# A fused linear-attention and gated-MLP layer on one core: state products in runs of four token tiles, and SBUF buffers cut into other sizes

## The chip, the core and the metric

The kernel runs on one core of one Trainium2 chip. The metric is the device time of one execution in microseconds (us). The core has five engines that run at the same time, each through its own instructions in order: TensorE (PE in the profile, its weight loads PEld), VectorE (DVE), ScalarE (ACT), GpSimd (POOL) and SyncE (SP, which here only issues DMA transfers). They wait for one another through semaphores.

## The reference, cut to what matters

One layer over x of 2048 tokens x 512 features (float32). A layer norm feeds two branches, whose product is added to x:

```
xn = layernorm(x)
q, k, v = xn @ wqkv                        # 32 heads of 16
phi(t) = [softmax(t @ w_phi), softmax(-t @ w_phi)]      # 32 features a head
kv = sum over tokens of phi(k)^T v;  z = sum over tokens of phi(k)
o  = phi(q) kv / (phi(q) z + 1e-6)
s  = o @ wo
gate, up = xn @ W_gate, xn @ W_up          # 1376 hidden features
h  = relu(gate) * up
out = x + s * silu(h @ W_down)
```

So no token's attention can be finished before the sums kv and z ("the state") over all 2048 tokens are complete.

## The kernel before, in words

**Tiles.** There are N = 16 token tiles of 128 tokens, numbered n in the order in which they are worked on (line 225: blocks 2 and 3 by turns, then 0 and 1). The kernel normalizes a tile (norm_*), turns it with TensorE (turn, transpose_x) and keeps it as two numbers of reduced precision, a high and a low part, in XT. Every large product is made of three: low x high, high x low, high x high (mm3, line 204). Products of two blocks are combined from sums of blocks (A11 to A22 and S1 to S4, line 48), so seven products do the work of eight.

**First part: keys, values, state.** Tiles 0 and 1 have code of their own (lines 1253 to 1293). Then pair(m) for m = 1 to 7 (line 1295) works on n = 2m and 2m + 1: key products (PSUM banks py and px, called pk in the profile; from pair 3 on `px` first takes a copy of `py`, the ACT instruction pk<-pk of line 1310, and TensorE writes on after it), value products (pv), the features of the keys (exponents, exp_all, features_k: subtract maxima, exp, sum, reciprocal, multiply; tile ek), the query products of a tile (query, line 421, bank pq; stored to DRAM as pq<-pqs), and in each pair the *state products* of the two tiles before, n - 2 and n - 1 (kv_products, lines 1376 to 1378 and 512). kv_products takes 16 small products for one tile, each on a quarter of the array (tile_position, 32 columns), all into one PSUM bank, PKV (pkv). Its operands ek and v can be written over only after it. features_split also adds ek to a sum in DRAM with a POOL DMA (zacc<-ek). After pair 7, state() (line 1426) takes the products of the last two tiles, copies the bank (kvacc, ACT), turns it (DVE) and spreads it into kvt.

**Second part: the hidden features.** The hidden size is cut into 11 feature tiles f. f_prep(f) (line 557) takes the raw weights of one tile (rawg, rawd, loaded by f_load, line 535: three DMAs on SP), forms their sums on POOL (tab), rounds high parts on ACT (wa, wb, wc, wd, fdh) and takes low parts on POOL, and stores all nine tiles to DRAM (put, ws<-...) for the second half of the tokens. At its end it loads the next tile's raw weights (line 611). gate_up_apart and gate_up (lines 757 and 708) make the seven block products of one feature tile; down makes the products with W_down. Two halves of 1024 tokens run one after the other. Between these products, q_pair and q_back work through the queries: stored queries are loaded from DRAM (q_load, line 851, tiles pql), turned, exponentiated and multiplied with the state (bank pnum). One column of query products (q_tile, line 640) uses weight sums that POOL and ACT make in q_sums (line 616) during pair 3 and 4. Last come the products with wo (out_tile).

**What sets the order.** Each engine's instructions keep the order in which the program issues them. The order of side work (f_prep, q_sums, all_queries, stores through pace.when) comes from Clock (line 68): it estimates when TensorE and the other engines are free, and pump() issues the next step of a generator when its operands should be there. f_prep(0) starts at pair 7, f_prep(1) after it (START, line 40); all_queries, which begins with state(), starts 30 blocks after the pairs (line 1502). PLAN (line 39) sets by hand where weight sums are made. SP issues DMAs in order: one that waits holds all behind it.

**Buffers.** SBUF tiles come from three sets that the whole kernel shares: u8 (8 KB a partition, B8 = 3), u4 (4 KB, B4 = 8) and u2 (2 KB, B2 = 40; line 31). A tile gets a buffer that is free, or its first writer waits until one is. In u8: the raw weights wkT, wvr, wqT, then th, rq, tq, the results y of two blocks, of2. In u4: zacc, ek, two weight sums, eq and ez of the queries, o and of. In u2: the attention weights, xt, v, and the feature tiles.

Of the kernel before, what the change touches and what calls it, by code (L numbers as in the profile page):

```python
# [13 lines left out]
P = 128  # L14
S = 2048
D = 512
# [3 lines left out]
KD = D // P  # L20
NF = -(-F // P)
# [4 lines left out]
NP = 8  # L26
CHUNKS = [(0, 1), (2, 3), (4, 5), (6, 7), (8, 9, 10)]
PAIRS = [(2, 3), (0, 1)]
B8, B4, B2 = 3, 8, 40
LEAD = 3  # L30
QUERIES = [(0, 1, 2), (6, 7, 4, 5, 3)]

# [7 lines left out]

START = (14, 15)
TURN = 9
KV_END = ()
SUMS = 5
WO_WITH = (4, 5, 6, 7)
DOWNS = {2: 1, 4: 1, 6: 1, 7: 1}
# [118 lines left out]
def layer_kernel(ctx: ExitStack, tc: tile.TileContext, x, wkT, wqT, wv, wo, wf, cst, out):  # L165
    pace = Clock()
    nc = InOrder(tc, pace)
# [81 lines left out]
    def fold_queries(*ks):  # L249

        ps_ = [ps((P, 2, KD, 64), name="pfold") for _ in range(2)]
        for i, k in enumerate(ks):
            for j in range(KD):
                for r in range(2):
                    rr = slice(64 * r, 64 * r + 64)
                    nc.tensor.matmul(ps_[r][:, i, j, :], wq_raw[rr, k, j * P:(j + 1) * P], bd_sb[rr, j, rr],
                                     start=i == 0 and j == 0, stop=True, skip_group_check=True, tile_position=(64 * r, 0))

        def parts(k):
            for r in range(2):  # L260
                split(*(t.rearrange("p (j r x) -> p r j x", r=2, x=64)[:, r] for t in WQ[k]), ps_[r][:, ks.index(k)])
        return [lambda k=k: parts(k) for k in ks]
# [246 lines left out]
            nc.sync.dma_start(to, flat(phi))  # L509
        PHI[n] = phi  # L510

    def kv_products(n):

        phi, v = PHI.pop(n).rearrange("p (j a c) s f -> p c j a (s f)", a=2, c=4), VH.pop(n)
        v = v.rearrange("p (c j x) -> p c j x", c=4, j=4)
        if n == 0:
            PKV.append(ps((P, 8, 64), name="pkv"))
        for j in range(4):
            for c in range(4):
                r = slice(32 * c, 32 * c + 32)  # L520
                nc.tensor.matmul(PKV[0][r, j], v[:, c, j], phi[:, c, j], start=n == 0 and j == 0,
                                 stop=n == N - 1, skip_group_check=True, tile_position=(0, 32 * c))
# [31 lines left out]
    def put(f, i, t):  # L554
        pace.when(t, lambda: nc.sync.dma_start(wspill[f][i], f32(flat3(t))))

    def f_prep(f, keep=True):


        rg, rd, tab = RAW.pop(f)  # L560
        b11, b12, b21, b22 = (rg[c][:, :, s, :] for c in range(2) for s in range(2))
        ta, tb = tab or two("tab", True)
        yield "gpsimd", b22
        add(nc.gpsimd, tb[:, 0], b12, b11, ALU.subtract)
        add(nc.gpsimd, ta[:, 1], b22, b12, ALU.subtract)
        if keep:
            wa, wb = w_pair("wa"), None
        else:
            t = u8((P, 4, 2, 2, P), "wab", F32R)
            wa, wb = (t[:, 0], t[:, 1]), (t[:, 2], t[:, 3])  # L570
        yield "scalar", b11
        for c in range(2):
            nc.scalar.activation(wa[0][:, c], rg[c][:, :, 0, :], AF.Copy)
        put(f, 0, wa[0])
        yield "gpsimd", ta
        add(nc.gpsimd, ta[:, 0], b22, tb[:, 0], ALU.subtract)
        add(nc.gpsimd, tb[:, 1], b21, ta[:, 0], ALU.subtract)
        wb = wb or w_pair("wb")
        yield "scalar", ta
        nc.scalar.activation(wb[0], ta, AF.Copy)  # L580
        put(f, 2, wb[0])
        for c in range(2):
            yield from sums_of(wa[1][:, c], rg[c][:, :, 0, :], f32(wa[0][:, c]), ALU.subtract, wa[0])
        put(f, 1, wa[1])
        wc = w_pair("wc")
        yield "scalar", tb
        nc.scalar.activation(wc[0], tb, AF.Copy)
        put(f, 4, wc[0])
        yield from sums_of(wb[1], ta, f32(wb[0]), ALU.subtract, wb[0])
        put(f, 3, wb[1])  # L590
        wd = u2((P, 2, 2, P), "wd", F32R)
        yield "scalar", b22
        nc.scalar.activation(wd[:, 0], b22, AF.Copy)
        yield from sums_of(wc[1], tb, f32(wc[0]), ALU.subtract, wc[0])
        put(f, 5, wc[1])
        fd = u2((P, D), "fdh", F32R), u2((P, D), "fdl", F32R)
        yield "scalar", rd
        nc.scalar.activation(fd[0], rd, AF.Copy)
        put(f, 7, fd[0])
        yield "gpsimd", wd  # L600
        add(nc.gpsimd, wd[:, 1], b22, f32(wd[:, 0]), ALU.subtract)
        put(f, 6, wd)
        yield from sums_of(fd[1], rd, f32(fd[0]), ALU.subtract, fd[0])
        put(f, 8, fd[1])
        if keep:
            FT[f], WD[f] = [wa, wb, wc, wd], fd
            nxt = f + 1
            while nxt in AHEAD:
                nxt += 1
            del rg, rd, ta, tb, tab  # L610
            if nxt < NF:
                f_load(nxt)
        DONE.add(f)
        yield None,

    def q_sums(q):

        t = u8((P, 4, 2, 2, P), "rq")
        r, ta, tb = [t[:, k] for k in range(2)], t[:, 2], t[:, 3]
        for k in range(KD):  # L620
            h, l = (f32(x[:, 256 * q:256 * q + 256].rearrange("p (d x) -> p d x", d=2)) for x in WQ[k])
            yield "gpsimd", WQ[k][1]
            add(nc.gpsimd, r[k // 2][:, k % 2], h, l)
        b11, b12, b21, b22 = (t[:, :, d, :] for t in r for d in range(2))
        o = u8((P, 2, 2, 2, 2, P), "tq", F32R)
        yield "gpsimd", r[1]
        add(nc.gpsimd, tb[:, 0], b12, b11, ALU.subtract)
        add(nc.gpsimd, ta[:, 1], b22, b12, ALU.subtract)
        yield "gpsimd", ta
        add(nc.gpsimd, ta[:, 0], b22, tb[:, 0], ALU.subtract)  # L630
        add(nc.gpsimd, tb[:, 1], b21, ta[:, 0], ALU.subtract)
        for i, x in enumerate((ta, tb)):
            yield "scalar", x
            nc.scalar.activation(o[:, i, 0], x, AF.Copy)
            yield from sums_of(o[:, i, 1], x, f32(o[:, i, 0]), ALU.subtract, o)
        TQ[q] = o
# [366 lines left out]
    def o_load(q):  # L1003
        LOADED.add(q)
        for u, parts in enumerate(UNITS):
            if q in [part[0] for part in parts]:
                pace.finish(BACK[u])
                for g in STORES.pop(u, []):
                    pace.finish(g)
        qs = QUERIES[q > QUERIES[0][-1]]  # L1010
        if q == qs[0]:

            t = u8((P, 2, 4, 256), "of2")
            OF[q], OF[qs[1]] = t[:, 0], t[:, 1]
            del t
        if q not in OF:
            OF[q] = u4((P, 4, 256), "of")
        nc.sync.dma_start(OF[q], OD[q])
        for t in (2 * q, 2 * q + 1):
            if t in yspill:  # L1020
                YK[t] = u2((P, D), "yk")
                nc.sync.dma_start(YK[t], yspill[t])
# [65 lines left out]
        return t  # L1088


    wk_raw, wv_raw, wq_raw = u8((P, KD, D), "wkT"), u8((P, KD, D), "wvr"), u8((P, KD, D), "wqT")
    bd_sb = u2((P, KD, P), "cb")
    ident = sb.tile([P, P], F32, name="ident")
    load_x(0)
# [20 lines left out]
        add(nc.gpsimd, by_parity(WV[k][1]), even_first(wv_raw[:, k, :]), f32(by_parity(WV[k][0])), ALU.subtract)  # L1115
    norm_vector(0)

    nc.vector.memset(wq_raw[:, 0, 0:1], 0.0)
    nc.sync.dma_start(wq_raw[:, 0:2, :], wqT[:, 0:2, :])
    nc.sync.dma_start(wv_raw[:, 0:2, :], wv[:, 0:2, :])  # L1120
    nc.sync.dma_start(wq_raw[:, 2:4, :], wqT[:, 2:4, :])
    load_x(2)
    nc.sync.dma_start(wv_raw[:, 2:4, :], wv[:, 2:4, :])
    for n in range(3, 7):
# [170 lines left out]
    def pair(m):  # L1295
# [77 lines left out]
        pace.pump()  # L1373
        features_split(n)
        t_steps(m, "split a")
        if m not in KV_END:
            kv_products(n - 2)
            kv_products(n - 1)
        pace.pump()
        if seven:  # L1380
            block(px, A22, T[3], False)
# [17 lines left out]
        if not seven:  # L1399
            features_v(n, va)  # L1400
        EB.append((eb, px))
        if m in KV_END:
            kv_products(n - 2)
            kv_products(n - 1)
        query(n)
        t_steps(m, "end")
        pace.pump()

    EB, MULT = [], [(None, None), (nc.gpsimd, nc.gpsimd)]
    for m in range(1, NP):  # L1410
        pair(m)
# [7 lines left out]
    nc.vector.memset(ones, 1.0)  # L1419
    kvt = sb.tile([P, NG, 32], F32, tag="kvt", bufs=1, name="kvt")  # L1420
    nc.vector.memset(kvt, 0.0)
    q_load(0)
    query(N - 1)
    pace.pump()

    def state():
        nonlocal kvacc
        kv_products(N - 2)
        kv_products(N - 1)

        kvacc = u2((P, 256), "kvacc")
        nc.scalar.activation(kvacc, PKV[0][:, :4].rearrange("p j x -> p (j x)"), AF.Copy)
        yield "vector", kvacc
        kvT = ps((P, 256), name="kvT")
        nc.vector.transpose(kvT, kvacc)
        kvT = kvT.rearrange("p (j x f) -> p j x f", x=4, f=DH)
        kvacc = None
        for c in range(4):
            r, h = slice(32 * c, 32 * c + 32), c % 2
            nc.vector.tensor_copy(kvt[r, :, DH * h:DH * h + DH].rearrange("p (j a) f -> p j a f", a=2), kvT[r, :, 0:4:3, :])  # L1440
        yield None,
# [22 lines left out]
    def all_queries(half):  # L1464
        nonlocal zs
        if not half:
            yield from state()
            zs = pace.add(normalizers(), first=True)
            yield 24,
        for u, parts in enumerate(UNITS):  # L1470
            if parts[0][0] in QUERIES[half]:
# [161 lines left out]
```

## Time and profile before

| | |
|---|---|
| median of 3 runs | 546.84 us (546.66 to 548.46) |
| the profiled execution's own time | 546.74 us |
| its span, first to last instruction | 545.0 us |
| granted TensorE clock | 1.00 |
| PE busy | 539.6 us (99%) |
| DVE, POOL, ACT busy | 372.4, 366.9, 258.7 us |
| moved by DMA | 125.98 MB |

How to read the lines: a group's or a timeline's row names the engine, the operation, what it writes <- what it reads by the program's tile names, the shape, and xN for N instructions. Numbers in front of it in the timeline are the start and the length in us from the span's start; [0.56 <-ACT pk] is idle time of that engine before the row and what ended it, inferred from semaphores. L64 is the helper through which every instruction is issued, so tiles identify the work. Matmuls overlap in the pipeline: their length is more than the distance between two starts, and the starts tell the pace.

### The profile page before, as it was taken

Reading aid. Unit: us, or ns where it says so; the run is one execution under the profiler, and the core shown is the slowest. Engines: PE = TensorE matmul, PEld = TensorE weight load, DVE = VectorE, ACT = ScalarE, POOL = GpSimd, SP = SyncE. Lnnn points to the kernel's source line nnn. Section 1 sums busy time; section 2 is a strip of 40 time slices with the busy share of each in tenths; the row PEclk is TensorE's granted clock in tenths of the full one; section 3 lists DMA queues with packets and bytes.
Section 4 is the critical chain, followed back from the end, with each engine's and each line's share of the span. In section 5 each row is a group of like instructions: output and inputs, shape, how many; then the busy total and the mean of one; then the engine's idle time right before and its main releaser. Section 6 shows DMA issues by size and latency. Waiting matters only on the chain.

```text
span 545.0 us, 9140 instructions
## 1 busy us (share of the span) xinstructions
PE 539.6 (99%) x3186; PEld 440.5 (81%) x3186; DVE 372.4 (68%) x585; ACT 258.7 (47%) x462; POOL 366.9 (67%) x328
## 2 busy tenths in 40 slices
PE   9999999999999999999999999999999999999997
PEld 8898888877887888787887888887777887878886
DVE  5988778677768338789883442899999494924323
ACT  3788767654435564545434240334354545342510
POOL 1569999767787999899896235262365765842591
PEclk9999999999999999999999999999999999999999
DMA  8339789555899957887869998692664735657073
GB/s 283 147 129 326 177 215 237 133 131 107 197 284 391 334 179 275 301 298 272 289 242 337 412 414 313 240 366 73 223 200 135 275 112 166 221 186 277 0 233 115
DMA packets 76367, 125.98 MB, mean 231 GB/s; under 512 B 6689, under 2 KB 29089, under 8 KB 75425
## 3 DMA queue, kind: packets, MB, share of 16 engines
q1 hardware_dynamic: 74160, 117.99, 61.7%
q0 software_dynamic: 2016, 7.34, 7.7%
q8 instruction: 25, 0.41, 0.3%
q14 instruction: 22, 0.17, 0.1%
q10 hardware_dynamic: 144, 0.07, 0.0%
HBM read 68.49 MB, written 52.69 MB: 222 GB/s over the span
## 4 chain that ended last, share of the span: by engine, by line
PE 90%; DVE 6%; issue 1%; DMA 1%; POOL 1%; ACT 0%; DVEq 0%; POOLq 0%; ACTq 0%
PE py L64 20%; PE pd L64 10%; PE pa L64 10%; PE pk L64 9%; PE pb L64 9%; PE pso L64 8%; PE pc L64 6%; PE pq L64 6%; PE pv L64 5%; PE pkv L64 2%; PE pfold L64 1%; PE pnum L64 1%; PE pxT L64 1%; DVE qs L64 1%; DMA wb<-ws 1%
## 5 line engine op out<-in xcount | busy, mean ns | idle before, releaser
L64 PE MATMUL py<-fdh,hl 128*128 128x512 f32 x176 | 69.1, 392 | 0.0
L64 PE MATMUL py<-fdl,hh 128*128 128x512 f32 x176 | 68.5, 389 | 0.0
L64 PE MATMUL py<-fdh,hh 128*128 128x512 f32 x176 | 68.5, 389 | 0.0
L64 PE MATMUL pa<-XT,wa 128*128 128x512 f32 x264 | 67.3, 390 | 0.0
L64 PEld LDWEIGHTS pa<-XT,wa 128*128 128x128 f32 x264 | 49.4, 188 | 11.1 <-POOL tab L64 0.4
L64 DVE TENSOR_TENSOR y<-py,y 128x512 f32<-128x512 f32 x40 | 27.5, 689 | 31.4 <-PE py L64 31.3
L64 POOL TENSOR_TENSOR hl<-t,hh 128x512 fp32r<-128x512 f32 x16 | 20.7, 1295 | 39.5 <-ACT hh L64 39.5
L64 POOL TENSOR_TENSOR y<-y,ys 128x512 f32<-128x512 f32 x24 | 30.9, 1292 | 17.9 <-ACT ys L64 17.4
L64 PEld LDWEIGHTS py<-fdh,hl 128*128 128x128 f32 x176 | 33.0, 188 | 8.8 <-issue 1.2
L64 PEld LDWEIGHTS py<-fdh,hh 128*128 128x128 f32 x176 | 33.0, 188 | 6.9
L64 POOL TENSOR_TENSOR ez<-eq,zB 128x1024 f32<-128x1024 f32 x16 | 38.5, 2412 | 0.1
L64 PEld LDWEIGHTS py<-fdl,hh 128*128 128x128 f32 x176 | 33.0, 188 | 6.7
L64 PE MATMUL pd<-XT,wd 128*128 128x512 f32 x132 | 33.9, 392 | 0.2
L64 PE MATMUL pd<-XT,wc 128*128 128x512 f32 x132 | 33.9, 391 | 0.0
L64 PE MATMUL pb<-XT,wb 128*128 128x512 f32 x132 | 33.6, 390 | 0.0
L64 POOL TENSOR_TENSOR ol<-of,oh 128x512 fp32r<-128x512 f32 (+1 forms) x13 | 19.8, 1548 | 20.3 <-ACT oh L64 20.3
L64 ACT ACTIVATE hh<-t 128x512 fp32r<-128x512 f32 x16 | 10.1, 633 | 49.3 <-DVE t L64 48.1
L64 PE MATMUL pc<-XT,wb 128*128 128x512 f32 x132 | 33.5, 389 | 0.0
L64 DVE TENSOR_REDUCE mx<-pk 128x32 f32<-128x512 f32 x32 | 20.5, 683 | 16.6 <-PE pk L64 16.5
L64 PE MATMUL pq<-XT,wqh 128*128 128x512 f32 (+1 forms) x112 | 30.6, 360 | 0.0
L64 DVE TENSOR_TENSOR pb<-pb,t 128x512 f32<-128x512 f32 x16 | 11.1, 696 | 28.4 <-ACT pd L64 28.3
L64 PE MATMUL pk<-wkh,XT 128*128 128x512 f32 x88 | 30.3, 396 | 0.0
(203 smaller groups left out, 1456.6 us busy)
## 6 DMA issues: line engine op xcount, KB each, us to landing
xts<-XT SPq DMA_DIRECT2D x4, 1792.0 KB
zacc<-ek POOLq DMA_DIRECT2D x14, 512.0 KB, 5.5
XT<-xts SPq DMA_DIRECT2D x7, 1024.0 KB
rawg<-wf SPq DMA_DIRECT2D x22, 256.0 KB
ws<-wa SPq DMA_DIRECT2D x22, 256.0 KB
ws<-wb SPq DMA_DIRECT2D x22, 256.0 KB
ws<-wc SPq DMA_DIRECT2D x22, 256.0 KB
wa<-ws SPq DMA_DIRECT2D x22, 256.0 KB
```

The lines of the kernel that those rows point to most:

```text
L64: return self.tc.keep_in_program_order(op(*a, **k))
```

## The change

It has four parts.

1. KV_AT = (2, 4, 6) replaces KV_END = (). The state products are taken only in pairs 2, 4 and 6, there for all tiles since the last time (four), and in state() for the last four. KV_FROM holds the first tile not yet taken.
2. Buffers: u8 from 3 to 2, u4 from 8 to 10, u2 stays 40; 56 KB in both. The raw query weights wqT become two u4 tiles of half the size, rq with its sums (q_sums) becomes two u4 tiles, and the first two tiles of loaded attention output in each half (of2) become two u4 tiles.
3. f_load(1) is issued inside f_prep(0), behind the store of the first rounded weights, no longer at its end.
4. q_load(0), which stood ahead of query(N - 1) and so ahead of state(), stands behind state() and the start of normalizers().

```
-B8, B4, B2 = 3, 8, 40
+B8, B4, B2 = 2,10,40
-KV_END = ()
+KV_AT = (2,4,6)
...
-                    nc.tensor.matmul(ps_[r][:, i, j, :], wq_raw[rr, k, j * P:(j + 1) * P], bd_sb[rr, j, rr],
+                    nc.tensor.matmul(ps_[r][:, i, j, :], wq_raw[k // 2][rr, k % 2, j * P:(j + 1) * P], bd_sb[rr, j, rr],
...
-    def kv_products(n):
+    def kv_products(*ns):
+        for n in ns:
+            kv_product(n)
+
+    def kv_product(n):
...
         put(f, 0, wa[0])
+        if f == 0:
+            f_load(1)
...
-            if nxt < NF:
+            if nxt < NF and nxt not in RAW:
                 f_load(nxt)
...
-        t = u8((P, 4, 2, 2, P), "rq")
-        r, ta, tb = [t[:, k] for k in range(2)], t[:, 2], t[:, 3]
+        r, (ta, tb) = (two(x, False) for x in ("rq", "tab"))
...
-            t = u8((P, 2, 4, 256), "of2")
-            OF[q], OF[qs[1]] = t[:, 0], t[:, 1]
-            del t
+            for k in qs[:2]:
+                OF[k] = u4((P, 4, 256), "of")
...
-    wk_raw, wv_raw, wq_raw = u8((P, KD, D), "wkT"), u8((P, KD, D), "wvr"), u8((P, KD, D), "wqT")
+    wk_raw, wv_raw, wq_raw = u8((P, KD, D), "wkT"), u8((P, KD, D), "wvr"), [u4((P, 2, D), "wqT") for _ in range(2)]
...
-        if m not in KV_END:
-            kv_products(n - 2)
-            kv_products(n - 1)
+        if m in KV_AT:
+            kv_products(*range(KV_FROM.pop(), n))
+            KV_FROM.append(n)
...
-        if m in KV_END:
-            kv_products(n - 2)
-            kv_products(n - 1)
...
-    q_load(0)
     query(N - 1)
...
     def state():
         nonlocal kvacc
-        kv_products(N - 2)
-        kv_products(N - 1)
+        kv_products(*range(KV_FROM[0], N))
...
             yield from state()
             zs = pace.add(normalizers(), first=True)
+            q_load(0)
             yield 24,
```

More of the change, by code (lines that the diff above doesn't have):

```diff
@@ L1116, in layer_kernel @@
     norm_vector(0)
-    nc.vector.memset(wq_raw[:, 0, 0:1], 0.0)
-    nc.sync.dma_start(wq_raw[:, 0:2, :], wqT[:, 0:2, :])
+    nc.vector.memset(wq_raw[0][:, 0, 0:1], 0.0)
+    nc.sync.dma_start(wq_raw[0], wqT[:, 0:2, :])
     nc.sync.dma_start(wv_raw[:, 0:2, :], wv[:, 0:2, :])
-    nc.sync.dma_start(wq_raw[:, 2:4, :], wqT[:, 2:4, :])
+    nc.sync.dma_start(wq_raw[1], wqT[:, 2:4, :])
     load_x(2)
@@ L1407, in pair @@
         pace.pump()
+    KV_FROM = [0]
     EB, MULT = [], [(None, None), (nc.gpsimd, nc.gpsimd)]
```

## The prediction

> **What bounds the kernel now.** I read the page first, its span and the engines' totals.
>
> ```profile
> span 545.0 us, 9140 instructions
> PE 539.6 (99%) x3186; PEld 440.5 (81%) x3186; DVE 372.4 (68%) x585; ACT 258.7 (47%) x462; POOL 366.9 (67%) x328
> ```
>
> TensorE is the bound, nearly without a gap, and the change takes no matrix product away. So it can win only what TensorE loses between products: at a change of tile shape, or at a short wait for another engine. To find those I read the waits of the weight loads, then everything that touches the state's bank pkv.
>
> ```profile
> PEld pkv L64 <- issue: 2.6, 8, 0.4
> PEld pd L64 <- DVE t L64: 1.0, 2, 0.5
> PEld pk L64 <- ACT pk L64: 0.8, 2, 0.6
> ```
>
> The largest entry is the state product itself: eight times, once before each run of small products, the weight load sits idle with nothing to wait for. A run is 64 records (two for each of 32 products) for two token tiles. All other waits are under 0.6 us.
>
> **Part 1: eight runs become four.** KV_AT = (2, 4, 6) leaves out the runs of pairs 1, 3, 5 and 7; those of pairs 2, 4, 6 and of state() take four tiles. The number of products stays; four times less TensorE goes into and out of them. The price of one such passage is in the timeline of TensorE around the first run:
>
> ```profile
> 39.19 0.40 PE L64 MATMUL pq<-XT,wqh 128*128 128x256 f32 x2
> 39.52 1.10 PE L64 MATMUL pkv<-ek,v 128*32 128x64 f32 x64
> 40.55 0.50 PE L64 MATMUL pk<-wkh,XT 128*128 128x512 f32 x1
> 40.89 0.40 PE L64 MATMUL pk<-wkl,XT 128*128 128x512 f32 x1
> 41.13 0.63 PE L64 MATMUL pk<-wkh,XT 128*128 128x512 f32 x2
> ```
>
> The pq products before start every 0.12 us (the row of two lasts 0.40, one of them 0.28), the last at 39.31, so the next start was due at 39.43 and came at 39.52: 0.09 lost. From the first to the last start of the run are 1.10 - 0.22 = 0.88 us for 63 steps, 0.014 each; at that pace the next start was due at 40.42 and came at 40.55: 0.13 lost. The first pk product then holds its successor for 0.34 instead of 0.24: 0.10 lost. Sum 0.32. The chain, in order of time, gives the same with other numbers (pair 4's run):
>
> ```profile
> 95.28 1.03 PE pkv L64 x64
> 96.31 1.58 PE pk L64 x6
> 97.89 1.36 PE pv L64 x6
> ```
>
> 1.03 against 64 x 0.014 = 0.90 is 0.13, and six products in 1.58 instead of 1.36 are 0.22: 0.35. I take 0.34, four times: **-1.36 us**. Bounds: the least is that only the entry goes and the exit grows with the run, 4 x 0.09 = 0.4 us; the most is 4 x 0.35 = 1.4.
>
> The Trainium skill has a rule that speaks against part of this: "TensorE: Matmul & The Clock Gate", section "The cost: per-tile semaphore tail", says that the tail behind a pack of tiled products grows by some 26 ns with each one that signals a semaphore. Two more signalling products in each of the four longer runs would give back about 0.2 us by that estimate. All runs here have the same length, so no row shows it.
>
> **Part 2: where the moved products land.** The 0.90 us of products taken out of pairs 1, 3, 5, 7 are done one pair later. That is neutral where TensorE is the bound, but not at its two waits for ACT (pk<-pk copies a key block aside before TensorE may write on):
>
> ```profile
> 133.21 0.58 ACT L64 ACTIVATE pk<-pk 128x512 f32<-128x512 f32 x1
> 133.32 0.39 PE L64 MATMUL pv<-h,XT 128*128 128x512 f32 x1
> 133.84 0.19 PEld L64 LDWEIGHTS pk<-h,XT 128*128 128x128 f32 x1 [0.56 <-ACT pk L64]
> 133.84 0.50 PE L64 MATMUL pk<-h,XT 128*128 128x512 f32 x1
> 134.18 0.40 PE L64 MATMUL pk<-l,XT 128*128 128x512 f32 x1
> ```
>
> From 133.32 to 133.84 are 0.52 us instead of 0.227 (6 products in 1.36), and the next step is 0.34: 0.29 + 0.11 = 0.40 lost. ACT is late because the exponents before it on ACT come from DVE, and in this stretch DVE has little idle time:
>
> ```profile
> 122.00:134.00 12.00, 11.87 (x114) 9.48 (x113) 10.70 (x17) 6.06 (x10) 8.28 (x9) 1.00 0.43 78
> ```
>
> (PE 11.87, PEld 9.48, DVE 10.70 us busy of 12.) Pair 6's run lies in this stretch and gets two tiles more, 0.90 us of work for TensorE exactly where it waits 0.29 us later. The wait is filled: **-0.40**. The bounds are -0.40 and 0.
>
> The other side is pairs 3, 5 and 7, which get 1.24 us shorter (0.90 + 0.34): ACT and DVE must follow. At the start of pair 6 they just keep up now:
>
> ```profile
> 115.11 1.29 DVE L64 TENSOR_REDUCE mx<-pk 128x32 f32<-128x512 f32 x2 [0.82 <-PE pk L64]
> 118.83 0.60 ACT L64 ACTIVATE pk<-pk 128x512 f32<-128x512 f32 x1
> 119.25 0.39 PE L64 MATMUL pv<-h,XT 128*128 128x512 f32 x1
> 119.48 0.50 PE L64 MATMUL pk<-h,XT 128*128 128x512 f32 x1
> ```
>
> TensorE starts at 119.48, one regular step after 119.25, with the copy done at 119.43. With TensorE 1.24 us earlier, DVE can begin mx only 0.82 earlier (its idle time), so exponents and copy come 0.8 to 1.0 earlier: a new wait of 0.2 to 0.4, of which I take **+0.2**. At pair 4 the copy has more room:
>
> ```profile
> 86.68 0.58 ACT L64 ACTIVATE pk<-pk 128x512 f32<-128x512 f32 x1 [0.47 <-PE pk L64]
> ```
>
> ACT idles 0.47 there, and TensorE has a block of 1.36 us between what the copy reads and what waits for it: 0 to 0.2, I take **+0.1**. In pair 7 DVE idles longer before it and nothing is added.
>
> **Part 3: the second feature tile's raw weights.** f_load(1) moves from the end of f_prep(0) to behind its first store. Its three DMA issues leave SP here and go behind ws<-wa:
>
> ```profile
> 133.57 0.45 SPq L64 DMA_DIRECT2D ws<-wa  x1
> 141.01 0.32 SPq L64 DMA_DIRECT2D ws<-wb  x1
> ...
> 144.31 2.78 SPq L64 DMA_DIRECT2D pql<-pq  x2
> ...
> 149.11 1.64 SPq L64 DMA_DIRECT2D rawg<-wf  x2
> ```
>
> SP issues nothing from 134.0 to 141.0; two issues of 1.64 us together and a third of half of that fit there, so the new place costs nothing (without that cover: some 2.5 us later stores, which nobody reads before the second half). What it gains shows one stage on:
>
> ```profile
> 154.66 1.44 POOL L64 TENSOR_TENSOR tab<-rawg 128x256 f32<-128x256 f32 x2 [0.98 <-DMA rawg<-wf]
> 156.84 0.63 ACT L64 ACTIVATE wb<-tab 128x512 fp32r<-128x512 f32 x1 [0.88 <-POOL tab L64]
> 159.02 0.58 ACT L64 ACTIVATE t<-pa 128x512 f32<-128x512 f32 x1
> 161.09 0.72 DVE L64 STREAM_TRANSPOSE pq<-pql 128x512 f32<-128x512 f32 x1
> 162.32 1.52 PE L64 MATMUL pc<-XT,wc 128*128 128x512 f32 x6
> 163.05 0.68 DVE L64 TENSOR_TENSOR e<-pd,e 128x512 f32<-128x512 f32 x1
> 163.84 1.22 PEld L64 LDWEIGHTS pd<-XT,wd 128*128 128x128 f32 x6 [0.43 <-POOL fdl L64]
> 163.88 1.63 PE L64 MATMUL pd<-XT,wd 128*128 128x512 f32 x6
> ```
>
> POOL waits 0.98 for the transfer. Its sums feed ACT's roundings of that tile; wb waits 0.88 for them and stands with others in front of t<-pa. That copy comes at 159.02, DVE follows, and its e<-pd is done at 163.73, where TensorE needs pd: due at 162.32 + 6 x 0.227 = 163.68, started at 163.88, and 1.63 instead of 1.52 for six. The row names POOL's fdl, but that never touches pd; what reads pd before it is written again is DVE's e<-pd. With the preparation 1 us earlier, e<-pd is done by about 162.7 and the wait of 0.20 + 0.11 goes: **-0.3** (0 if another DVE step is pushed in front).
>
> **Part 4: the stored queries.** q_load(0) leaves SP's 144.31 and goes behind the state's copies, near 153 to 156 on SP (between ws<-wd and zodd). DVE reads it at 161.09, so 5 to 8 us are left for two loads of 256 KB. The nearest rows are rawg's, two of 256 KB too: issued from 149.11, waited for by POOL until 154.66, 5.5 us. Taken: 0. If the loads are late, DVE stands at the transpose with e<-pd behind it, and TensorE behind that: up to +1.
>
> **Part 5: buffers.** u8 loses one buffer (8 KB), u4 gains two (4 KB each). wqT becomes two u4, rq and tab take two u4, of2 becomes two u4. I counted what lives: u4 holds at most zacc, h0, l0, five ek, rq and tab, ten of ten, in pair 4. The two u8 hold wkT and wvr, then th and tq, then two y; the second half's first y is written two feature tiles (14 blocks of 1.36 us) after the first half's last use. So 0 for these. The tight one is u2, unchanged at 40: in the middle of pair 4 live 28 weights and weight sums, four xt, three v, and by turns junk, va, vb, xf, sb, pqs, about 40; v will live longer, two more at a time, about 42 for 40. Allocations there wait for the run that frees v. DVE's sb is the one that matters:
>
> ```profile
> 94.48 0.42 DVE L64 TENSOR_TENSOR sb<-xf,pxT 128x256 f32<-128x256 f32 x1
> 97.93 1.29 DVE L64 TENSOR_REDUCE mx<-pk 128x32 f32<-128x512 f32 x2 [0.71 <-PE pk L64]
> ```
>
> If sb waits until the first tile of pair 4's run (95.28, above) is done, 0.25 later, DVE and what is queued on it (sb, sm, rc, then POOL's ek and ACT's XT) come 1.0 us later, and DVE has 0.71 idle before it next follows TensorE. I take 0 on TensorE; the upper bound is below.
>
> **Sum.** -1.36 - 0.40 + 0.2 + 0.1 - 0.3 = -1.76. The profiled execution took 546.74 us (span 545.0 and 1.7 around it); the median of the runs shown is 546.84, so its own time stands for it. 546.74 - 1.76 = 545.0. A measurement here tells about 0.3% (1.64 us) from no change: below 545.2 is faster, above 548.5 slower. The forecast lies just beyond that line.
>
> **Rivals.** *Only the passages go*: the small waits stay or come back elsewhere, since ACT and DVE set them and their order of work shifts. For it: waits of this size follow from DVE's order, and pairs 3 to 6 give ACT little room. Against: the filled wait at 133.8 needs nothing but TensorE being later. 546.74 - 1.36 + 0.2 = 545.6.
>
> *The exit grows with the run*: twice the length, twice the 0.13 us of each exit, four times: 546.1. No row speaks for it, since all runs are alike; against it, the steps within a run do not lengthen (0.88 us for 63). The Trainium skill's rule of the semaphore tail, in the section named above, would make an exit grow so, though less.
>
> *DVE stands still for a buffer*: sb in pairs 2 and 4 gets the last v of the run rather than the first, and waits from 94.48 to the run's end (95.28 + 1.9 = 97.2), 2.7 us, less 0.7 idle: 2.0 in pair 4 and, taken alike, in pair 2. That is 546.74 - 1.36 + 4.0 = 549.4, slower. It decides from the point where each of the two reaches TensorE with 0.7 us: then the 1.36 are gone. Against it: the first freed buffer is at hand 1.7 us before the last.
>
> *More than forecast*: without the new waits in pairs 4 and 6, and with one of the later waits (DVE t, 2 x 0.5) gone by the shifted order, 544.2.
>
> **Chances.** Forecast 0.45, only the passages 0.30, a growing exit 0.05, more 0.12, DVE's buffer 0.08. Of the forecast's case about three quarters lie below 545.2, of the second a seventh: faster 0.50, same 0.42, slower 0.08. The range 544.0 to 546.4 takes in the first four cases, the second up to a passage priced at its least (546.74 - 0.4 = 546.3), and leaves out the last.
>
> **What would show it.** The tile view of pkv: 512 records in four runs of 128 and four idle times of 0.3 instead of eight; a run of about 1.93 us in the chain. No wait for ACT pk near 133 and a small one near 118. No wait of POOL or ACT for rawg near 154, and no wait before pd<-XT,wd near 162. I am wrong if a run of 128 lasts clearly over 1.95, if sb waits for TensorE in pairs 2 or 4, if the transpose pq<-pql waits for its DMA, or if new waits appear in the feature tiles after 165.

## The result, and the profile after

The changed kernel took 545.25 us (median of 16 executions, 544.78 to 546.56) against 547.0 us for the kernel before (16, 546.37 to 549.0): ratio 0.9965, interval 0.9956 to 0.9974, so 1.4 to 2.4 us faster, about 1.8. Measured a second time it took 545.56 against 547.36, ratio 0.9969 (0.9959 to 0.9980). The forecast was 545.0. One execution of the variant kv_only below took 1362.5 us and is left out of its ratio; all others agree with their kernel's median within 0.5%.

The page of the kernel after, span and engine totals:

```profile
span 543.6 us, 9136 instructions
PE 538.3 (99%) x3186; PEld 441.1 (81%) x3186; DVE 372.2 (68%) x585; ACT 258.8 (48%) x462; POOL 366.8 (67%) x328
```

As many products as before; the span is 1.4 shorter. This execution's first products came 0.4 later than those of the profile of before. Other profiles differ in this by up to 1.4 us, so what follows compares stages.

The waits of TensorE's weight loads after (sum, times, longest):

```profile
PEld pkv L64 <- issue: 1.6, 5, 0.4
PEld pk L64 <- ACT pk L64: 0.9, 2, 0.6
```

The idle times at the bank pkv fell from eight to five, 2.6 to 1.6. Four of the five stand before the four runs, one before the later products with `ones`; of the eight before, that one and seven before runs (the first run had none). The wait for ACT's pk has about the same sum (0.9, before 0.8) but has moved, as shown below. The chain after, at pair 4's run:

```profile
94.75 1.92 PE pkv L64 x128
96.67 1.58 PE pk L64 x6
98.25 1.36 PE pv L64 x6
```

128 records take 1.92 = 128 x 0.014 + 0.13: what is left over is the 0.13 of a run of 64, and the six products behind lose 0.22 as before. The exit doesn't grow with the run. That is where the Trainium skill ("TensorE: Matmul & The Clock Gate", section "The cost: per-tile semaphore tail") would have 0.05 more for each longer run, by an estimate from its 26 ns; in this trace the start of the next product shows the exits equal to 0.01.

Near 133, TensorE and ACT in the timeline after:

```profile
132.46 0.58 ACT L64 ACTIVATE pk<-pk 128x512 f32<-128x512 f32 x1
133.40 0.39 PE L64 MATMUL pv<-h,XT 128*128 128x512 f32 x1
133.62 0.39 PE L64 MATMUL pk<-h,XT 128*128 128x512 f32 x1
133.85 0.39 PE L64 MATMUL pk<-l,XT 128*128 128x512 f32 x1
```

The copy ends at 133.04, before TensorE needs it, and the starts are 0.23 apart: the 0.40 lost there before are gone. So is the wait before pd<-XT,wd:

```profile
161.61 1.52 PE L64 MATMUL pc<-XT,wc 128*128 128x512 f32 x6
162.97 1.52 PE L64 MATMUL pd<-XT,wd 128*128 128x512 f32 x6
```

The two are 1.36 apart, a block's length; before, 0.28 more were lost here. A second small wait went with it, at py<-fdh,hl near 179.4. The kernel before had there:

```profile
179.31 0.39 PE L64 MATMUL py<-fdh,hh 128*128 128x512 f32 x1
179.63 0.50 PE L64 MATMUL py<-fdh,hl 128*128 128x512 f32 x1
```

The step from 179.31 is 0.32 instead of 0.23, and the next was 0.34: 0.09 + 0.11 lost.

The new waits stand in pairs 3 and 4. First a weight load of pair 3, then the timeline of pair 4:

```profile
78.93 0.30 PEld L64 LDWEIGHTS pk<-th,XT 128*128 128x128 f32 x2 [0.36 <-POOL th L64]
```

```profile
86.51 0.60 ACT L64 ACTIVATE pk<-pk 128x512 f32<-128x512 f32 x1
86.58 0.39 PE L64 MATMUL pv<-h,XT 128*128 128x512 f32 x1
87.16 0.50 PE L64 MATMUL pk<-h,XT 128*128 128x512 f32 x1 [0.19 <-ACT pk L64]
```

Pair 3 loses 0.21 at products that read th. In pair 4 the step from 86.58 is 0.58 instead of 0.23, and the next 0.33: 0.46 lost. A third, of 0.08, is at the start of pair 6.

**The account**, all on TensorE: passages -1.36, the wait at 133 -0.40, those at 163 and 179 -0.48, pair 3 +0.21, pair 4 +0.46, pair 6 +0.08: -1.5. The medians give -1.8, and the interval of 1.4 to 2.4 us takes the -1.5 in.

### The profile page after: what moved, and what is told of

The parts are those of the page before. It is cut to its first block, busy times and chain, and to the rows that moved or that the text cites. A ratio compares the mean times of both kernels' runs of the same rounds, so it can differ in the third digit from the quotient of the medians.

```text
span 543.6 us, 9136 instructions
## 1 busy us (share of the span) xinstructions
PE 538.3 (99%) x3186; PEld 441.1 (81%) x3186; DVE 372.2 (68%) x585; ACT 258.8 (48%) x462; POOL 366.8 (67%) x328
## 4 chain that ended last, share of the span: by engine, by line
PE 89%; DVE 6%; POOL 2%; issue 2%; ACT 1%; ACTq 0%; DVEq 0%; POOLq 0%
PE py L64 20%; PE pd L64 10%; PE pa L64 10%; PE pb L64 9%; PE pso L64 8%; PE pk L64 8%; PE pc L64 7%; PE pv L64 5%; PE pq L64 5%; PE pkv L64 2%; PE pfold L64 1%; PE pnum L64 1%; PE pxT L64 1%; DVE qs L64 1%; PE pidle L64 1%
## 5 line engine op out<-in xcount | busy, mean ns | idle before, releaser
L64 PEld LDWEIGHTS pd<-XT,wd 128*128 128x128 f32 x132 | 24.6, 188 | 6.0 <-DVE t L64 1.0
```

The lines of the kernel that those rows point to most:

```text
L64: return self.tc.keep_in_program_order(op(*a, **k))
```

## The experiments

Two theories stood at first. *Separate gains*: passages, filled waits and the early load each pay by themselves, the buffers and the late q_load give nothing. *Buffers and loads*: the gain comes from parts 2 to 4. The first result fitted neither, and led to a third: *held together*, the merged runs alone run into something that another part takes away. Ratios are to the kernel before, measured beside each variant (547.21, 547.09 or 547.36 us).

**Part 1 alone** (kv_only): buffers 3, 8, 40, and both loads where they were.

```
-KV_END = ()
+KV_AT = (2, 4, 6)
...
+        if m in KV_AT:
+            kv_products(*range(KV_FROM.pop(), n))
+            KV_FROM.append(n)
```

> The kernel before with part 1 alone: state products in pairs 2, 4, 6 and four tiles in state(); buffers 3/8/40, loads where they were. Theory (passages): four passages of 0.34 us go (-1.36), the wait for ACT pk near 133 goes (-0.40), small new waits in pairs 3, 4 and 6 take back 0.3 to 0.7: 1.1 to 1.5 us below the kernel before, and the wait before pd<-XT,wd near 163 (0.2 to 0.3 us) is still there. Rival (the gain is in buffers and loads): within 0.5 us of the kernel before.

Measured: 551.6 us, ratio 1.0080 (1.0066 to 1.0094): 4.4 us slower. The expectation fell, and *separate gains* with it; so did the rival, which had the time within 0.5 us. The four passages and the filled wait near 133 are in this trace as in that of the kernel after, the pair-4 wait too; the loss comes later. TensorE in the timeline:

```profile
157.03 1.52 PE L64 MATMUL pc<-XT,wb 128*128 128x512 f32 x6
162.02 2.93 PE L64 MATMUL pd<-XT,wc 128*128 128x512 f32 x6 [3.47 <-DVE kvt L64]
164.75 2.76 PE L64 MATMUL pa<-XT,wa 128*128 128x512 f32 x6
167.31 1.89 PE L64 MATMUL pc<-XT,wc 128*128 128x512 f32 x6
```

pd was due at 158.39 and started at 162.02, 3.6 late; the next two blocks took 2.73 and 2.56 instead of 1.36. Together 6.2 us. pd takes over the PSUM bank of kvT, so it needs DVE's copies into kvt. What these waited for is on ACT:

```profile
158.98 0.42 ACT L64 ACTIVATE wa<-rawg 128x256 fp32r<-128x256 f32 x1 [8.74 <-DMA rawg<-wf]
159.88 0.37 ACT L64 ACTIVATE kvacc<-pkv 128x256 f32<-128x256 f32 x1
```

kvacc, the copy of the finished state, stands behind the rounding of the second feature tile's raw weights, and those came 9.1 us after their issue. SP shows why they were issued late:

```profile
143.28 0.76 SPq L64 DMA_DIRECT2D pq<-pqs  x1
147.84 0.32 SPq L64 DMA_DIRECT2D pql<-pq  x1
149.84 0.89 SPq L64 DMA_DIRECT2D rawg<-wf  x2
```

The second of the two loads of q_load(0) reads what the pq store before it writes; SP stands at it from 144.0 to 147.8, and rawg is queued behind. What then slowed the transfer shows the DMA view from 150 to 155 us (the queue's packets, MB, share of the 16 engines), first of kv_only, then of the kernel before:

```profile
q0 software_dynamic: 136, 0.51, 58.7%
```

```profile
q0 software_dynamic: 15, 0.04, 10.2%
```

q0 carries POOL's accumulate zacc<-ek (it adds a tile to a sum in DRAM), here of the last token tile. In kv_only POOL issued it at 148.69, ahead of rawg, and it took more than half of the engines' time just then; before, it was issued at 150.80, behind rawg, which landed in 5.5 us.

**Part 1 and part 3** (kv_load), so q_load and the buffers stay:

```
         put(f, 0, wa[0])
+        if f == 0:
+            f_load(1)
...
-            if nxt < NF:
+            if nxt < NF and nxt not in RAW:
```

> Parts 1 and 3 without the other two: merged state products and the early load, buffers 3/8/40, q_load(0) ahead of the state. The run with part 1 alone was 4.4 us above the kernel before: ACT stood 8.7 us at the second feature tile's raw weights, with the state's copy behind it, and TensorE stood 3.6 us and then ran at half clock for some 5 us. Theory (the late raw load is what turns the merge into a loss): with the early load ACT no longer stands there, and the time is that of the changed kernel, 1.5 to 2.0 us below the kernel before. Rival (the buffers 2/10/40 or the late query load are what make the merge pay): still 2 us or more above the kernel before.

Measured: 545.45 us, ratio 0.9972 (0.9960 to 0.9983). The early load turns a loss of 4.4 into a gain of 1.6, and the buffers aren't needed for it.

**Everything but part 3** (no_load): the two lines of f_load(1) taken out of the kernel after.

> The changed kernel without the early load (f_load(1) back at the end of f_prep(0)); merge, buffers and late q_load(0) stay. Theory (the late raw load): ACT and POOL wait for rawg again with the state's copy kvacc behind, TensorE waits before pd<-XT: at least 0.5 us above the changed kernel, and 3 to 5 us above the kernel before if the load lands as late as it did with part 1 alone. Rival (buffers or late query load): within 0.5 us of the changed kernel.

Measured: 545.36 us, ratio 0.9970 (0.9960 to 0.9981), the same as the kernel after. A miss: the loss didn't come back. SP and ACT of this kernel:

```profile
146.93 0.92 SPq L64 DMA_DIRECT2D rawg<-wf  x2
149.34 2.03 SPq L64 DMA_DIRECT2D pql<-pq  x2
```

```profile
153.22 0.42 ACT L64 ACTIVATE wa<-rawg 128x256 fp32r<-128x256 f32 x1 [1.66 <-DMA rawg<-wf]
154.11 0.37 ACT L64 ACTIVATE kvacc<-pkv 128x256 f32<-128x256 f32 x1
```

With q_load behind them the raw weights are issued 2.9 us earlier than in kv_only, and ahead of the accumulate (150.00 in this trace). They land in 6.3 and hold kvacc back only to 154.1. TensorE doesn't notice. Parts 3 and 4 thus cover the same trouble twice. (The new buffers are in this run too; no run has the merge with part 4 alone or with the buffers alone.)

**Part 1 with the accumulate issued later** (kv_zlate), to separate the accumulate from SP's order:

```
-    features_split(N - 1)
+    PHI[N - 1] = EK.pop(N - 1)
...
     def state():
...
+        last = PHI[N - 1]
         kv_products(*range(KV_FROM[0], N))
...
+        nc.gpsimd.dma_start(zacc2, flat(last), accum_op=ALU.add)
         yield None,
```

> The kernel before with the merged runs alone (as in kv_only), and the accumulate of the last token tile into DRAM (zacc2<-ek, 512 KB, on POOL) issued behind the copies into kvt, no longer ahead of the second feature tile's loads. In kv_only the loads of rawg took from 149.84 to 158.96, 9.1 us, and in that stretch the software queue of that accumulate (issued at 148.69) moved 0.52 MB against 0.11 MB in the kernel before, where the accumulate was issued at 150.80, behind the loads. Theory that the accumulate's transfer goes ahead of the raw weights': rawg lands in 5 to 6.5 us, ACT's wa<-rawg does not hold kvacc back, TensorE does not stand at 158, and the time is 545.3 to 546.5. Rival, the loads are late because SP issues them behind the stored queries' loads: 551 as in kv_only. An opposite risk is that the normalizers (pkv<-zodd) come some us later, which nobody reads before the first pnum products.

Measured: 549.45 us, ratio 1.0044 (1.0031 to 1.0058). That is neither the theory's 545.3 to 546.5 nor the rival's 551. The transfer did as expected, the time did not. ACT, and TensorE:

```profile
155.21 0.42 ACT L64 ACTIVATE wa<-rawg 128x256 fp32r<-128x256 f32 x1 [8.68 <-DMA rawg<-wf]
156.44 0.42 ACT L64 ACTIVATE wa<-rawg 128x256 fp32r<-128x256 f32 x1 [0.81 <-DMA rawg<-wf]
158.00 0.63 ACT L64 ACTIVATE wb<-tab 128x512 fp32r<-128x512 f32 x1 [0.66 <-POOL tab L64]
158.54 0.37 ACT L64 ACTIVATE kvacc<-pkv 128x256 f32<-128x256 f32 x1
```

```profile
160.68 1.65 PE L64 MATMUL pd<-XT,wc 128*128 128x512 f32 x6 [1.13 <-DVE kvt L64]
165.35 1.65 PE L64 MATMUL pc<-XT,wc 128*128 128x512 f32 x6 [1.64 <-DVE e L64]
```

Issued at 150.05, about as late as in kv_only, the first of the loads landed after 5.2 us instead of 9.1: the accumulate did hold them up. But the edit also changed the order on ACT. Here kvacc stands behind wb, which waits for POOL's sums until 158.00; in kv_only it stands ahead of wb, 0.3 behind the start of the second wa. TensorE stood 1.3 and 1.8 us, and 1.1 more near 202 (for POOL's wa), and 2.1 of the 4.4 us remain. With kvacc at kv_only's place it would have started near 156.8, and pd, which follows it by 2.1, near 158.9, before it was due at 159.4. By this estimate the accumulate alone makes the first stand, and SP's late issue matters because it puts the loads behind the accumulate. No run shows that, because the order differs here; what the late issue costs by itself is open. The two later stands weren't followed further.

**Parts 2 to 4 of the diff without the merge** (rest_only: the kernel after with KV_AT = (1, 2, 3, 4, 5, 6, 7)).

> The changed kernel with the state products back in every pair (eight runs): buffers 2/10/40, early load and late query load stay. Theory (passages): only the wait near 163 goes, 0.3 us below the kernel before; the wait for ACT pk near 133 stays. Rival (buffers and loads): 1.3 to 1.9 us below, as the changed kernel.

**Part 3 alone** (load_only: the kernel before with the lines of kv_load).

> The kernel before with the early load of the second feature tile alone. Theory: POOL and ACT no longer wait for rawg near 154, e<-pd comes before TensorE needs pd, the wait near 163 goes: 0.3 us below the kernel before. Rival (the wait comes from the query work that stands in front of e<-pd on DVE, not from the load): the wait near 163 stays within 0.1 us, time unchanged.

Measured: rest_only 546.32 us, ratio 0.9989 (0.9980 to 0.9998); load_only 546.25 us, 0.9988 (0.9979 to 0.9997). Both gain some 0.1 to 1.1 us, which takes in the 0.3 of both theories and leaves out rest_only's rival (1.3 to 1.9). TensorE of load_only:

```profile
162.24 1.52 PE L64 MATMUL pc<-XT,wc 128*128 128x512 f32 x6
163.60 1.52 PE L64 MATMUL pd<-XT,wd 128*128 128x512 f32 x6
```

1.36 apart: the wait is gone, and the one near 179 too, 0.48 in all, while the wait near 133 stays (0.29 + 0.11) in both traces. So the early load removes the first two, and the merge the third. (The first two are gone in no_load as well, so the early load is one way to remove them, not the only one.)

**The runs split instead of merged** (kv_split): fifteen passages instead of eight.

```
-            kv_products(n - 2)
-            kv_products(n - 1)
+        kv_products(n - 2)
...
         eb = exponents(px)
+        kv_products(n - 1)
```

> The kernel before with each pair's two state products taken apart: the second tile's run stands behind the next key block, so 15 passages into and out of the small products instead of 8, the same 256 products. Theory (passages): 7 x 0.34 = 2.4 us above the kernel before, give or take 0.4 of small waits; runs of 32 records with the same entry and exit as runs of 64. Rival (the cost goes with the number of products, or ACT and DVE set the time): within 0.5 us of the kernel before.

Measured: 548.51 us, ratio 1.0027 (1.0015 to 1.0039): +1.5, less than the 2.0 to 2.8 expected. The chain of this kernel:

```profile
39.45 0.58 PE pkv L64 x32
```

0.58 = 32 x 0.014 + 0.13: a run of 32 leaves the same 0.13 over as one of 64 or 128. Seven more passages at 0.34 are 2.4. The missing 0.9 are the waits near 133, 163 and 179 (0.40, 0.28, 0.20), all gone from this trace, since TensorE came later to them. So a small wait for a late engine can be filled by a loss ahead of it.

**Two u2 buffers for one u4** (b2_42): the kernel after with 2, 9, 42.

```
-B8, B4, B2 = 2,10,40
+B8, B4, B2 = 2, 9, 42
```

> The changed kernel with one u4 buffer cut into two u2 (2/9/42). In the changed kernel two waits are left in pairs 3 and 4 (th: 0.1 + 0.1 us, the copy pk<-pk: 0.35 + 0.1 us), and ACT's vb stands 1.3 us in pair 3 until POOL's th frees a buffer, DVE's v 1.8 us in pair 4. Theory (u2 is short, these are waits for a buffer): with 42 the waits of vb and v go, th is not late, and 0.2 to 0.6 us come off the changed kernel. Rival (ACT and DVE are simply behind, since TensorE comes 1.2 us earlier): both waits of TensorE stay within 0.1 us, time unchanged; or the ninth u4 is missed and DVE waits for ek.

> The changed kernel with buffers 2, 9 and 42, once more, beside the changed kernel itself. If the two u2 buffers are what removes the waits of pairs 3 and 4 (0.21 and 0.46 us) it is 0.7 to 1.0 below the changed kernel of the same call: 544.2 to 544.6 against 545.2. Rival, the difference between the two calls was chance: the two agree within 0.3.

> The changed kernel once more, to stand beside b2_42_again: 545.2, within 0.4, with the waits at the start of pairs 3 and 4 (0.21 and 0.46 us) in its trace again.

Measured: 544.28 us, ratio 0.9952 (0.9938 to 0.9965); with the kernel after beside it, 544.29 against 545.56, ratios 0.9953 (0.9939 to 0.9966) and 0.9969 (0.9959 to 0.9980). The difference is 1.3 us by the medians and 0.9 by the ratios, whose intervals overlap; the rows are clearer. Both traces of the kernel after have the waits of pairs 3 and 4, neither trace of 2, 9, 42 has them. ACT and TensorE at the start of pair 4:

```profile
84.98 0.58 ACT L64 ACTIVATE pk<-pk 128x512 f32<-128x512 f32 x1
85.92 0.39 PE L64 MATMUL pv<-h,XT 128*128 128x512 f32 x1
86.14 0.39 PE L64 MATMUL pk<-h,XT 128*128 128x512 f32 x1
```

The copy is done 0.6 before it is needed, and the products of pair 3 have no wait either. What made ACT late in the kernel after stands in pair 3; ACT's vb, first of the kernel after, then of b2_42:

```profile
76.31 0.60 ACT L64 ACTIVATE vb<-pk 128x512 f32<-128x512 f32 x1 [1.31 <-POOL th L64]
```

```profile
74.50 0.60 ACT L64 ACTIVATE vb<-pk 128x512 f32<-128x512 f32 x1
```

vb is a u2 tile, and it waited for a POOL instruction that doesn't make its operand: for a buffer. With 42 it doesn't wait. DVE's v, a u2 tile too, waited 1.8 in pair 4 of the kernel after and doesn't with 42. (In the kernel before vb waited 1.04, and TensorE, at that point later, didn't notice. Whether 42 would gain there wasn't run.) This is the fastest version of the study, some 1 us under the kernel after and 3 under the kernel before.

**A longer run still** (b2_42_136: 2, 9, 42 and KV_AT = (1, 3, 6), so six token tiles in pair 6).

> Buffers 2/9/42 and the state products in pairs 1, 3, 6 (two, four and six tiles) and four in state(): four passages as in the changed kernel, but pairs 3 and 6 hold TensorE longer, just where it waits for th and pk<-pk. Theory (passages, and products placed where TensorE waits anyway): the waits of pair 3 and at the start of pair 4 go, 0.4 to 0.7 us below the changed kernel; in pair 6 seven ek, zacc and two sums want ten u4 of nine, so DVE may wait there for a buffer until the run, up to +1. Rival (only the number of passages counts): as the changed kernel within 0.2 us.

Measured: 550.43 us, ratio 1.0061 (1.0049 to 1.0074): slower, a miss. TensorE in the timeline of pair 6:

```profile
122.26 2.53 PE L64 MATMUL pkv<-ek,v 128*32 128x64 f32 x162
128.11 0.65 PE L64 MATMUL pkv<-ek,v 128*32 128x64 f32 x30 [3.31 <-issue]
```

In the middle of the run TensorE stood for 3.3 us, for nothing that the profile shows: not for a buffer. Behind it the clock fell (last section), and near 69.5 a new wait costs 0.5. The stand could be a wait for code, that is for the instructions themselves. **The run cut in two** (b2_42_42) tests this:

```
-            kv_products(*range(KV_FROM.pop(), n))
+            kv_products(*range(KV_FROM.pop(), n - 2 * (m == 6)))
...
             px = project(n + 1, WK, "pk")
+        if m == 6:
+            kv_products(n - 2, n - 1)
```

> b2_42_136 (buffers 2, 9 and 42, runs in pairs 1, 3 and 6) with the run of six token tiles in pair 6 cut in two: four tiles at the old place, two behind the next key block. In b2_42_136 TensorE stood for 3.3 us after 162 records of that run with no semaphore to wait for, while one packet of 16 KB on the instruction queue arrived in the stand (at 125.7). Theory that the code of a run of 192 products (384 instructions with their weight loads, more than the 256 that one packet of 16 KB would hold at 64 bytes each) comes too late: the stand and the half clock behind it go, one passage (0.34) is added: 544.3 + 0.34 + 0.4 (the wait at 69.5) = 545.0, within 0.7. Rival, another engine or a buffer holds the products of the last two tiles back: the stand of 3 us stays in the second part, 549 to 550.5.

Measured: 547.77 us, ratio 1.0015 (1.0003 to 1.0027), 2.7 better but 2.8 above the expectation, and below the rival's 549. The stand is still there, shorter:

```profile
126.94 0.64 PE L64 MATMUL pkv<-ek,v 128*32 128x64 f32 x28
129.30 0.75 PE L64 MATMUL pkv<-ek,v 128*32 128x64 f32 x36 [1.72 <-issue]
```

The windows view up to the middle of each stand tells where TensorE stopped (window, length, busy time with the number of records, clock, DMA), first of b2_42_136, then of b2_42_42:

```profile
0.00:127.00 127.00, 123.35 (x980) 1.00 0.71 198
```

```profile
0.00:128.50 128.50, 125.25 (x980) 1.00 0.69 194
```

Both stopped after exactly 980 records. In b2_42_136 that is two records into the sixth tile of the run, in b2_42_42 inside the fifth: a place in the code, not in the data. The queue q8 brings code in packets of 16 KB, 25 in the whole span, one for every 127 of TensorE's records and as many weight loads; by this count it is taken for TensorE's. In the window from 100 to 125.5 us it brought one in the kernel after, two in b2_42, and none in b2_42_136 and b2_42_42. The kernel after:

```profile
q8 instruction: 1, 0.02, 0.3%
```

The missing packet came in the stand, from 124.8 to 128.1 in b2_42_136:

```profile
q8 instruction: 1, 0.02, 1.7%
```

The page "Runtime: NRT & Kernel Launch" of the Trainium skill, section "Instruction fetch mechanics", has instructions fetched in 16 KiB blocks of 256, the next while one runs, the cost mostly hidden. The packets agree; the cost here was 3.3 and 1.7 us. In b2_42_136 the packet lies between 125.7 and 126.65 us, in b2_42_42 between 126.9 and 127.9, and TensorE goes on 1.4 to 1.5 us behind the end of each. So a wait for code fits both stands in place, end and order, though no run moves the packet alone to prove it. The packet was already missing before the long run began, so the run's length alone isn't shown to be the cause; why it came late in these two kernels is open.

## Why the prediction was right

- **The passages, -1.36**: right in kind and size. Entry, exit and the slow step behind are the same for 32, 64 and 128 records, so the rival with the growing exit is out. The reading of the eight idle times was off by one: seven stand before runs, the eighth before the products with `ones`, so five remain and not four. (Nor were all other waits under 0.6: one of 1.1 stands at the start, which the change doesn't touch.)
- **The filled wait, -0.40**: right; it is the merge that fills it (the wait is there in rest_only and load_only, gone in kv_only).
- **The wait at pd, -0.3**: right, shown by load_only; with the wait near 179, which I hadn't counted, -0.48.
- **New waits, +0.2 in pair 6 and +0.1 in pair 4**: the kind right, the sizes wrong, 0.08 and 0.46. And pair 3 had one, 0.21, of which I said nothing.
- **Buffers, 0**: this step failed. "About 42 for 40" fits what b2_42 shows, but I put the shortage at sb, which stands behind v on DVE and didn't wait itself. It fell on vb in pair 3 and on v in pair 4, and 42 buffers remove the waits of pairs 3 and 4: the kernel pays 0.7 by rows, 0.9 to 1.3 by the times, for its two missing u2. My pair-4 term was in truth part of this one. (The delay of sb was also worked out wrong: the first tile of a run takes 32 x 0.014 = 0.45, not 0.25.)
- **The late q_load, 0 on SP between 153 and 156**: it was issued at 147.05, and the early load at 129.04, ahead of ws<-wa (132.79) and not behind it; both sooner than I said. Both cost 0, as forecast.
- **What the sum hid.** I added the parts as if each stood alone. Part 1 alone costs 4.4 us. The second feature tile's raw weights and the state's copy share ACT, and I saw the wait for rawg as a cause of small waits only, not as what stands in front of kvacc. The rows of the kernel after show how far that has been moved:

```profile
145.94 0.71 ACT L64 ACTIVATE wa<-rawg 128x256 fp32r<-128x256 f32 x2
152.16 0.38 ACT L64 ACTIVATE kvacc<-pkv 128x256 f32<-128x256 f32 x1 [1.42 <-PE pkv L64]
```

wa is rounded 5.5 us before the state is ready, and kvacc waits for TensorE alone. By rows the sum should have been -1.5: pairs 3 and 4 cost 0.57 more than I took, pair 6 0.12 less, and the waits at pd and py gave 0.18 more. That the forecast's -1.76 meets the -1.75 of the medians is therefore partly luck: these errors have both signs, and the rows account for -1.5.

The rival *only the passages* was wrong in its reason (the small waits did go), though its 545.6 is almost as near as the forecast: the two measurements of 545.25 and 545.56 don't tell them apart, only the rows do.

## What to carry to other kernels

Price a switch of tile shape once, from the starts around one run, and multiply: it held here at 0.34 us for runs of three lengths. When a part is costed at nothing because something hides it, ask what it hides in turn; two edits that seem idle may each be enough to keep a third from costing more than it gains. And count buffers by what allocates late, not by what is largest: two more small ones were worth half as much as the four passages by rows, and nearly as much by the medians.

## What the runs showed of the hardware

After the 3.6 us stand in kv_only TensorE ran at half its clock. The windows view of kv_only (window, length, busy times of the five engines with counts, then clock, DMA share, GB/s):

```profile
162.00:166.00 4.00, 3.98 (x9) 3.14 (x10) 3.33 (x6) 1.94 (x4) 4.00 (x6) 0.50 0.84 276
```

and that of b2_42_136 after its 3.3 us, for TensorE alone:

```profile
128.70:132.70 4.00, 4.00 (x14) 0.57 0.49 135
```

After stands of 1.3 to 1.9 us (kv_zlate, b2_42_42) the clock stayed at 1.00. This agrees with the Trainium skill, "TensorE: Matmul & The Clock Gate", section "Why this matters for your kernels", which warns of gaps over about 3 us. The long stand in kv_only cost its length and 2.6 us more.

The first of two loads of 256 KB landed in 5.2 to 6.3 us where the accumulate was issued behind it (5.5 in the kernel before, 6.3 in no_load, 5.2 in kv_zlate), and in 9.1 where the accumulate went ahead (kv_only).

The stands of b2_42_136 and b2_42_42 look like TensorE out of code: both after 980 records, with a 16 KB packet arriving in each, and nothing in the waits but "issue".
